# Masked attention weights in column blocks, a split copy of the first keys, and a new instruction list

## The chip, the cores and the metric

The kernel runs on one core of one Trainium2 chip. The metric is the device time of one execution in microseconds (us); lower is better. Five engines work side by side, each through its own instructions in program order: TensorE (PE in the profile; PEld are its weight loads), VectorE (DVE), ScalarE (ACT), GpSimd (POOL), and SyncE (SP), which issues most DMAs.

## The reference

A layer norm of x (2048 rows of 512) feeds two branches, whose outputs are added to x: an attention of 32 heads with a memory over four segments of 512 rows, and a dense layer with silu.

```python
xn = _layernorm(x, axis=-1)
return x + _A_ref(xn, A_wq, A_wk, A_wv, A_wo, A_beta) + _B_ref(xn, B_w1, B_w2)
# _A_ref, for each segment s of 4 (L = 512 rows, heads of 16 columns):
logits = jnp.einsum('bhqd,bhkd->bhqk', qs, ks) * scale + mask
p = _softmax(logits, axis=-1)
a_dot = jnp.einsum('bhqk,bhkd->bhqd', p, vs)
pq = phi(qs)
num = jnp.einsum('bhld,bhde->bhle', pq, M)
den = jnp.einsum('bhld,bhd->bhl', pq, z)[..., None] + 1e-06
o = g * (num / den) + (1.0 - g) * a_dot
pk = phi(ks)
M = M + jnp.einsum('bhld,bhle->bhde', pk, vs)
z = z + jnp.einsum('bhld->bhd', pk)
# _B_ref: silu(x @ w1) @ w2, with 1792 inner columns
```

The mask is `(row < column) * -1e9`: a query attends to keys up to its own row. phi(t) is t + 1 where t > 0, and exp(t) elsewhere.

## The kernel before

The whole program is one list of words, `ORDER`, written out by hand or by a search outside the kernel. Each word names a piece of work and is issued in that order; each engine then takes its own instructions in that order, held only by semaphores for data and buffers. `k0.1.2` is part 2 of the key product of segment 0, column tile 1; `q`, `v`, `h` and `o` (with the parts `oc`, `od`, `oh`) are the products of queries, values, the dense layer and the output. `S` is a batch of scores with its exponential and masks, `E` and `O` are the products of the weights with the values for the even and the odd half of each head pair. `ha` and `hv` are the tanh on ScalarE and the product on VectorE that make silu. In segments 0 and 1 a dense product of 512 columns has four parts of two matmuls of 256 columns, or of one of 512, about equal in length. These are the smallest pieces with which the list fills the time between two batches of scores.

Keys: `k_copy` (L370 on) copies the product of keys from PSUM to `kT` and then, on GpSimd, writes `k3`: the keys times a mask of the odd heads (512 columns) and, for half of the columns, of the even heads.

Scores: `scores` (L684 on) makes one of 72 batches. Nine batches serve each pair of column tiles in each segment. A batch holds one to two chunks, each a tile of 128 keys against all later queries, for four heads, and fills 512 columns of each of four PSUM banks (`psS`, of which there is one). One ScalarE operation (L707) writes the exponentials of all 2048 elements per partition as bf16 to a buffer `Pb`, of which six exist. GpSimd then sets to zero what the mask excludes (L718): for each chunk, the triangle of its first columns in place, and for the even half beforehand the lower rows of that triangle to a small buffer, `lows`.

```python
ONE = [[(0, 0, 0)], [(0, 0, 3), (0, 0, 1)], [(1, 0, 3), (1, 0, 0)], [(1, 0, 2), (1, 0, 1)]]
BATCHES = ONE + [[(0, 0, 2), (0, 1, 2)]] + [[(par, 1, kt) for par, _, kt in chunks] for chunks in ONE]
```

An entry is (half, tile of the pair, tile of keys). The lengths of the chunks are 512 - 128 kt columns in the even half and 64 less in the odd one. Batch 4 has two chunks of equal length, which one GpSimd operation masks; the two chunks of batches 1 to 3 and 6 to 8 differ in length and are masked one by one.

`weigh` (L746 on) multiplies the weights with the values (L763). As the next batch of scores writes the same four banks, its matmuls wait for the exponential of the batch before.

Prologue: four tiles of x are loaded, two on SyncE's and two on ScalarE's queue. Statistics on VectorE (L281, L284), a square root on ScalarE (L298) and a scaling (L310) give the normalized tile, which TensorE turns. 44 dummy matmuls (`busy44`, L836) and six more run meanwhile. `tb` (L304) loads ScalarE's table for the exponential ahead of its first use.

Of the kernel before, what the change touches and what calls it, by code (L numbers as in the profile page):

```python
# [8 lines left out]
AF = mybir.ActivationFunctionType  # L9
ALU = mybir.AluOpType  # L10
# [9 lines left out]
S1 Nv5 vv0.2 h0.5.0 h0.10.0 h0.10.1 h0.10.2 v0.3.3 vv0.3 xs8 Nv6 XD6 h0.5.1 h0.5.2 XD5 h0.5.3 ha0.5  # L20
S3 q0.3.0 q0.3.1 q0.3.2 q0.3.3 hv0.5 k0.2.0 qv0.3 Nv4 XD4 k0.2.1 k0.2.2 tanh h0.10.3 ha0.10
S4 fv0.0 k0.2.3 kv0.2 h0.11.0 h0.11.1 h0.11.2 h0.11.3 ha0.11 fv0.1 v1.3.0 v1.3.1 v1.3.2 v1.3.3
S7 vv1.3 hv0.10 h0.13.0 h0.13.1 fa0.3 h0.13.2 hv0.11 fp0.2 O0 E0 Ev0 Ov0
S5 v1.2.0 v1.2.1 v1.2.2 h0.13.3 ha0.13 v1.2.3 xs9 vv1.2 q1.1.0 q1.1.1 q1.1.2 q1.1.3 qv1.1 xs11
S11 Om0 v1.0.0 hv0.13 v1.1.0 v1.0.1 v1.0.2 v1.1.1 v1.0.3 h0.1.0 h0.1.1 h0.1.2 fp0.3 ga1.1
S6 vv1.0 v1.1.2 v1.1.3 xs10 lw0 xg8.4 h0.1.3 ha0.1 q1.2.0 t0.0 q1.2.1 q1.2.2 fv0.3 k1.2.0 vv1.1 k1.2.1 k1.2.2 k1.2.3 kv1.2
S8 q1.2.3 fa0.2 h0.2.0 h0.2.1 h0.2.2 h0.2.3 E1 qv1.2 gate hv0.1 h0.7.0
S9 q1.0.0 Ev1 fv0.2 t0.2 k1.1.0 k1.1.1 k1.1.2 Nv10 Nv11 h0.7.1 h0.7.2 h0.7.3 k1.1.3 kv1.1 ha0.7 hv0.7 q1.0.1 q1.0.2 Nv9 ha0.2 hv0.2
S10 h0.4.0 h0.4.1 XD10 t0.1 h0.4.2 h0.4.3 ha0.4 fp1.2 O1 Ov1 hv0.4 q1.0.3 h0.9.0 bmask qv1.0 gp1.0
S13 ga1.0 XD9 k1.3.0 h0.9.1 h0.9.2 k1.3.1 k1.3.2 xl0.2 h0.8.0 h0.8.1 xs13 h0.8.2 h0.8.3 k1.3.3 t0.3 kv1.3 ha0.8  # L30
S12 h0.12.0 h0.9.3 hv0.8 h0.12.1 h0.12.2 h0.12.3 ha0.12 k1.0.0 k1.0.1 XD11 k1.0.2 k1.0.3 Nv8 XD8 kv1.0 ha0.9 h1.11.0
S15 hv0.12 hv0.9 h1.11.1 h1.11.2 h1.11.3 ha1.11 E2 Ev2 O2 h1.9.0 h1.9.1
S17 Ov2 h1.9.2 h0.0.0 h0.0.1 hv1.11 o0.2.4 oc0.2.2.0 xs12 xs14 oc0.2.2.1 h1.9.3 ha1.9 hv1.9 o0.2.10 xs15 xg12.4 h0.0.2 oc0.2.9.1
S21 xl0.3 o0.2.1 q1.3.0 q1.3.1 o0.2.7 h0.0.3 q1.3.2 m0.2 ha0.0 o0.2.5 mv0.2 Om1 q1.3.3 qv1.3 hv0.0
S14 o0.2.11 h1.10.0 h1.10.1 gv1.0 Nv14 ga1.2 q2.1.0 o0.2.12 m0.0 mv0.0 q2.1.1
S16 qv2.1 h1.10.2 h1.10.3 gp1.2 h0.3.0 ha1.10 od0.2.0.2 h0.3.1 E3 h0.3.2 Ev3 h0.3.3 ha0.3 hv1.10
S19 hv0.3 h0.6.0 h0.6.1 h0.6.2 h0.6.3 ha0.6 O3 h1.0.0 Nv15 Ov3 h1.0.1 h1.0.2
S24 XD14 h1.0.3 k2.2.0 k2.2.1 Om2 hv0.6 v2.2.0 kv2.2 o0.2.3 gv1.2 oc0.2.9.0 sv0 ha1.0 hv1.0
S18 lw1 r0.1 v2.1.0 v2.1.1 r0.2 vv2.1 v2.2.1 vv2.2 o0.2.6 k2.1.0
S22 o0.2.13 k2.1.1 h1.8.0 kv2.1 h1.8.1 h1.5.0 h1.8.2 r0.0 h1.8.3 ha1.8 r0.3 XD15 w0 z0.0 h1.5.1  # L40
S20 z0.2 k2.0.0 hv1.8 z0.1 h1.5.2 h1.5.3 z0.3 gp1.1 k2.0.1 kv2.0 E4 Ev4 ha1.5 hv1.5 od0.2.0.3
S28 h1.4.0 h1.4.1 h1.4.2 q2.3.0 h1.4.3 ha1.4 q2.3.1 qv2.3 o0.0.9
S26 ga2.1 o0.0.1 oc0.0.13.0 od0.0.11.2 oc0.0.4.0 hv1.4 Nv12 O4 Ov4 q2.0.0 zv0.2 q2.0.1 qv2.0 zv0.0
S23 o0.0.2 XD12 h1.1.0 o0.0.16 h1.1.1 h1.1.2 od0.2.0.0 o0.2.16 h1.1.3 xl0.0 h1.12.0 ha1.1 od0.0.11.1 od0.0.11.0
S25 h1.12.1 h1.12.2 Om3 h1.12.3 od0.2.0.1 zv0.3 o0.0.14 oc0.0.4.1 hv1.1 gv1.1 o0.0.17 ha1.12 E5 Ev5 oc0.0.13.1
S29 o0.0.12 hv1.12 o0.0.8 od0.0.11.3 k2.3.0 zv0.1 k2.3.1 fa1.2 O5 kv2.3
S27 h1.6.0 mw0.0 fv1.2 o0.0.10 o0.0.6 t1.2 o0.0.5 gp2.1 h1.6.1 h1.6.2 o0.2.15 Ov5 h1.6.3 ha1.6 o0.0.0 hv1.6
S31 o0.0.7 o0.0.3 Nv13 XD13 o0.0.15 st0.0 o0.2.17 h1.13.0 h1.13.1 h1.13.2 h1.13.3 o0.2.8 ha1.13
S30 gv2.1 o0.1.17 od0.1.8.1 h1.3.0 h1.3.1 h1.3.2 h1.3.3 ha1.3 gp1.3 hv1.13 o0.1.6 od0.1.8.0 fp1.3 oc0.1.10.1 o0.1.3 hv1.3 o0.2.14 st0.2
S33 q2.2.0 oc0.1.10.0 o0.1.15 q2.2.1 qv2.2 o0.1.5 E6 fa1.3 fv1.3  # L50
S32 Ev6 o0.3.0 oc0.3.13.1 oc0.3.11.1 od0.3.10.3 oc0.3.11.0 o0.3.6 od0.1.8.2 o0.1.4 od0.3.10.2 mw0.2 Om5 od0.3.10.1 O6 t1.3 fa1.0 o0.3.15 Ov6
S35 od0.1.8.3 o0.1.13 oc0.3.13.0 o0.3.5 o0.3.12 o0.1.7 E7 Ev7 xl0.1 od0.3.10.0 ga1.3 oc0.1.12.0 o0.3.9 gv1.3 fp1.0 fv1.0 t1.0
S34 fp1.1 o0.1.0 v2.0.0 v2.0.1 vv2.0 h1.2.0 h1.2.1 fa2.3 o0.1.16 o0.3.17 Om6
S41 o0.3.8 o0.1.11 o0.1.1 O7 o0.1.14 oc0.1.12.1 fa1.1 o0.3.4 xl1.0 Ov7 o0.1.9
S37 o0.1.2 st0.1 h1.2.2 h1.2.3 o0.3.1 o0.3.3 o0.3.16 xl1.2 ha1.2 o1.2.4 od1.2.5.1 fv1.1 t1.1 m1.2 mv1.2 o1.2.1
S36 s1 hv1.2 o0.3.7 sv1 o0.3.2 fp2.0 r1.0 o0.3.14 st0.3 q3.1.0 q3.1.1 qv3.1 o1.2.12 fp2.3 fa2.0
S40 r1.1 v2.3.0 v2.3.1 vv2.3 h2.8.0 h2.8.1 r1.3 fv2.3 r1.2 ha2.8 hv2.8 q3.2.0
S43 q3.3.0 q3.3.1 qv3.3 w1 o1.2.8 q3.2.1 fa2.2 qv3.2 k3.1.0 d1.1 od1.2.5.2
S38 k3.1.1 kv3.1 z1.2 E8 Ev8 k3.0.0 k3.0.1 d1.2 m1.0 mv1.0
S42 h2.0.0 kv3.0 v3.3.0 xl1.1 od1.2.5.0 h2.0.1 ha2.0 v3.3.1 Om7 h1.7.0 fv2.0 vv3.3 d1.3  # L60
S39 fa2.1 hv2.0 h1.7.1 h1.7.2 h1.7.3 ha1.7 v3.0.0 v3.0.1 vv3.0 E9
# [32 lines left out]
def kernel(  # L94
# [820 lines left out]
```

## Time and profile before

| | |
|---|---|
| median of 3 runs | 222.32 us (222.01 to 222.53) |
| profiled execution | 222.15 us |
| its span | 220.4 us |
| granted TensorE clock, mean | 0.999 |
| exponentials (L707) | 72, 1878 ns each |
| masks on GpSimd (L718) | 120 in place, 56 to lows |

The span runs from the first to the last instruction; the profiled execution's own time is 1.75 us longer. A row of a timeline has the start, the length, the engine, the line, the operation and its operands (out<-in), how many instructions were merged (x), and in brackets how long the engine sat idle before it and what ended that. A row of the groups has the count, the busy time and the mean duration, and the idle time before. The lengths of matmuls overlap, since they are pipelined: their pace is read from start to start.

### The profile page before, as it was taken

What the parts mean: (1) busy time and instruction counts of PE and PEld (TensorE: products, weight loads), DVE (VectorE), ACT (ScalarE), POOL (GpSimd) and SP (SyncE); (2) the same over time, 40 slices, a digit from 0 to 9 for tenths busy, and PEclk for the clock granted to TensorE, in tenths of its full rate; (3) what the DMA queues carried; (4) which work ended last, traced back from release to release, by engine and by line L of the source; (5) the groups of instructions that cost most, each with busy time, mean ns of one, the idle gap of its engine ahead of it and who ended that gap; (6) DMA issues with size and microseconds to landing.
All of it is one profiled execution on the core that took longest, in us unless ns stands there. A gap on an engine that the chain in (4) does not pass through costs nothing.

```text
span 220.4 us, 9441 instructions
## 1 busy us (share of the span) xinstructions
PE 214.9 (97%) x4057; PEld 117.2 (53%) x4057; DVE 179.7 (82%) x368; ACT 184.0 (83%) x173; POOL 135.1 (61%) x253
## 2 busy tenths in 40 slices
PE   7999999999999999999999999999999999999994
PEld 7666645655553444454544444455454544455662
DVE  7789999988889788776897888969789887579554
ACT  3699999999999999999998999999989997971000
POOL 6089667997769976876669696693756364320000
PEclk9999999999999999999999999999999999999999
DMA  5993549552014221223303130142242020232313
GB/s 183 373 385 87 74 27 304 106 77 58 21 28 122 88 59 29 50 51 76 102 17 95 40 96 4 28 92 59 52 120 64 15 76 7 75 94 68 109 51 97
DMA packets 32746, 19.61 MB, mean 89 GB/s; under 512 B 14656, under 2 KB 32192, under 8 KB 32704
## 3 DMA queue, kind: packets, MB, share of 16 engines
q1 hardware_dynamic: 30080, 16.39, 28.6%
q10 hardware_dynamic: 2624, 2.62, 3.9%
q8 instruction: 31, 0.51, 1.0%
q14 instruction: 11, 0.09, 0.2%
HBM read 9.96 MB, written 2.10 MB: 55 GB/s over the span
## 4 chain that ended last, share of the span: by engine, by line
PE 79%; ACT 10%; DVE 4%; POOL 4%; issue 2%; POOLq 0%
PE ps L331 21%; PE psO L333 16%; PE ps L333 13%; PE psS L701 10%; PE psO L331 9%; ACT Pb L707 7%; PE psV L763 6%; PE psS L333 4%; POOL Pb L718 2%; DVE xn_t L310 1%; POOL lows L718 1%; ACT ex L408 1%; ACT th L477 1%; PE psM L437 1%; DVE stats L281 1%
## 5 line engine op out<-in xcount | busy, mean ns | idle before, releaser
L707 ACT ACTIVATE Pb<-psS 128x2048 bf16<-128x2048 f32 x72 | 135.2, 1878 | 7.5 <-PE psS L701 6.4
L718 POOL TENSOR_SCALAR_AFFINE_SELECT Pb<-Pb 128x256 bf16<-128x256 bf16 (+2 forms) x120 | 66.1, 571 | 22.3 <-ACT Pb L707 19.5
L482 DVE SCALAR_TENSOR_TENSOR hT<-th,ps 128x512 bf16<-128x512 bf16 x56 | 37.7, 679 | 9.1 <-ACT th L477 8.5
L718 POOL TENSOR_SCALAR_AFFINE_SELECT lows<-Pb 64x256 bf16<-64x256 bf16 (+1 forms) x56 | 26.7, 490 | 27.7 <-ACT Pb L707 25.3
L333 PE MATMUL psO<-w_sb,hT 128*32 128x512 bf16 (+2 forms) x716 | 42.5, 319 | 0.0
L331 PE MATMUL ps<-xnT,w_sb 128*128 128x512 bf16 (+1 forms) x160 | 35.2, 334 | 0.0
L477 ACT ACTIVATE th<-ps 128x512 bf16<-128x512 f32 x56 | 33.0, 598 | 2.2 <-PE ps L333 2.1
L333 PEld LDWEIGHTS <-hT 128*32 128x32 bf16 x884 | 21.8, 96 | 14.0 <-issue 3.3
L333 PE MATMUL ps<-xnT,w_sb 128*32 128x512 bf16 (+1 forms) x480 | 27.1, 341 | 0.1
L701 PE MATMUL psS<-qT,k 32*128 32x64 bf16 (+3 forms) x512 | 23.0, 233 | 0.8 <-ACT Pb L707 0.3
L331 PE MATMUL psO<-w_sb,hT 128*128 128x512 bf16 (+2 forms) x87 | 22.7, 334 | 0.0
L701 PEld LDWEIGHTS <-k 32*128 32x128 bf16 x512 | 9.8, 92 | 23.2 <-issue 21.7
L763 PE MATMUL psV<-Pb,Vz 128*32 128x448 bf16 (+7 forms) x512 | 21.6, 286 | 0.3 <-POOL Pb L718 0.3
L331 PEld LDWEIGHTS <-w_sb 128*128 128x128 bf16 x160 | 14.9, 98 | 12.1 <-issue 1.6
L763 PEld LDWEIGHTS <-Vz 128*32 128x32 bf16 x768 | 16.5, 97 | 9.1 <-issue 1.1
L376 POOL TENSOR_SCALAR k<-kT,pm_odd 128x512 bf16<-128x512 bf16 x16 | 12.0, 748 | 8.0 <-ACT kT L373 7.0
L333 PEld LDWEIGHTS <-w_sb 128*32 128x32 bf16 x480 | 11.9, 96 | 7.3 <-issue 1.9
L331 PE MATMUL ps<-wv_sb,xnT 128*128 128x512 bf16 x56 | 15.1, 381 | 0.2
L701 PE MATMUL psS<-qT,kT 16*128 16x448 bf16 (+3 forms) x256 | 14.7, 269 | 0.0
L333 PE MATMUL psO<-wo_sb,oT 128*32 128x512 bf16 x156 | 14.4, 380 | 0.0
L331 PE MATMUL ps<-xnT,wk_sb 128*128 128x256 bf16 (+1 forms) x64 | 13.6, 326 | 0.0
L793 DVE CAST oraw<-psV 128x512 bf16<-128x512 f32 x16 | 11.0, 689 | 3.0 <-PE psV L763 2.9
(110 smaller groups left out, 321.2 us busy)
## 6 DMA issues: line engine op xcount, KB each, us to landing
spr<-rz SPq DMA_DIRECT2D x56, 64.0 KB
x_res<-in_A_x_dram SPq DMA_DIRECT2D x16, 128.0 KB
out_dram<-o_out SPq DMA_DIRECT2D x15, 128.0 KB
w_sb<-in_B_w_dram SPq DMA_DIRECT2D x1, 1792.0 KB
w_sb<-in_B_w_dram ACTq DMA_DIRECT2D x1, 1792.0 KB
x_hi<-in_A_x_dram SPq DMA_DIRECT2D x2, 512.0 KB
wv_sb<-in_A_wv_dram SPq DMA_DIRECT2D x2, 256.0 KB
wk_sb<-in_A_wk_dram SPq DMA_DIRECT2D x1, 512.0 KB
```

What stands on the lines that cost most here:

```text
L281: nc.vector.bn_stats(out=stats[t][:], in_=xs(t, t + 1)[:, 0, :])
L310: eng.tensor_scalar(out=xn[t][:], in0=xs(t, t + 1)[:, 0, :], scalar1=mv_all[:, t, 0:1], scalar2=rstd_all[:, t, 0:1], op0=ALU.subtract, op1 ...
L331: return [nc.tensor.matmul(out, lhsT=lhsT, rhs=rhs, start=start, stop=stop, skip_group_check=True)]
L333: nc.tensor.matmul(out[c : c + 32], lhsT=lhsT[:, c : c + 32], rhs=rhs, start=start, stop=stop, tile_position=(0, c), skip_group_check=True,)
L376: nc.gpsimd.tensor_scalar(out=to, in0=frm, scalar1=keep[:, 0:1], scalar2=1.0, op0=ALU.mult, op1=ALU.mult)
L477: nc.scalar.activation(out=th[:], in_=sts[s]["h", ft][:, :], func=AF.Tanh, scale=0.5)
L482: nc.vector.scalar_tensor_tensor(out=st["hT"][:, ft, :], in0=st.pop(("th", ft))[:], scalar=1.0, in1=st.pop(("h", ft))[:, :], op0=ALU.add, ...
L701: nc.tensor.matmul(psS[:, g, c : c + q2 - q1], lhsT=keys[rows], rhs=st["qT"][rows, dt, q1:q2], start=True, stop=True, tile_position=(32 * ...
L707: exp = nc.scalar.activation(out=Pb[:, :, :], in_=psS[:, :, :], func=AF.Exp, scale=SCALE)
L718: over[id(Pb)].append(nc.gpsimd.affine_select(out=out, in_=in_, compare_op=ALU.is_ge, fill=0.0, base=base, pattern=[[0, out.shape[1]], [1, ...
L763: nc.tensor.matmul(psV[32 * g : 32 * g + 32, q0 : q0 + nq], lhsT=Vzs[s % 2][:, kt, 4 * dt + g, par : par + 2, :].rearrange("p a d -> p (a ...
L793: copy(out=oraw[:], in_=sts[s].pop(("psV", 0))[:, :])
```

## The change

1. Blocks. The weights of batches with two chunks of unlike length lie in `Pb` in blocks of columns, all four heads of a block together: 128 columns in batches 1 and 6, 64 in batches 2 and 7. The other batches stay as they are. The first blocks of the two chunks are then neighbours, and one GpSimd operation masks both (and one writes the lower parts of both). ScalarE writes the exponentials by blocks; the products with the values read them by blocks.
2. Prologue. Tile 0 of x is loaded in two halves on two queues. The small masks of odd and even heads are made later. The keys of tile 0 go through a new `k_fast`: ScalarE copies them, VectorE multiplies by the odd mask out of PSUM, and ScalarE multiplies half of them by the even mask out of PSUM. The table for the exponential is loaded earlier (`tb`), the first copy of queries moves to ScalarE, and 40 dummy matmuls replace 44.
3. The list `ORDER` is another one throughout.

```diff
-kind odd omask ones0 ones1 zeros xc0 xd0 xc1 xq0 xi0 Nv0 busy44 xd1 xq1 xc2 xi1 X0.1 Nv1 ... va0.0 va0.1 Nv3 Xv2.1 X3.1 Xv3.1 k0.0.0 k0.0.1 k0.1.0 k0.0.2 k0.0.3 k0.3.0 q0.0.0 q0.0.1 q0.0.2 q0.0.3 ka0.0 fp0.0 qv0.0 tb fa0.0 q0.2.0 k0.1.1 k0.1.2 k0.1.3 kv0.1 fp0.1
-S0 q0.1.0 q0.1.1 q0.1.2 q0.1.3 k0.3.1 xs4 xs6 xs7 xs5 xg4.4 q0.2.1 q0.2.2 qa0.1 q0.2.3 qv0.2
-S2 ...
+ones0 ones1 zeros xc0 xd0 xc1 xq0 xi0 Nv0 busy40 xd1 xq1 xc2 xi1 X0.1 Nv1 ... Nv2 X2.1 xi3 va0.0 Nv3 tb Xv2.1 X3.1 Xv3.1 k0.0.0 k0.0.1 odd kind va0.1 k0.3.0 k0.0.2 k0.0.3 kf0.0 q0.0.0 q0.0.1 q0.0.2 q0.0.3 qa0.0 k0.3.1 fa0.0 k0.3.2 k0.3.3
+S0 v0.3.0 q0.3.0 q0.3.1 q0.3.2 xs5 xs6 xs7 xs4 xg4.4 k0.1.0 k0.1.1 k0.1.2 k0.1.3 ka0.1 q0.3.3 qv0.3
+S2 ...
...
-    load_x(nc.sync, 0, 1)
+    load_x(nc.sync, 0, 1, slice(0, P // 2))
+    load_x(nc.scalar, 0, 1, slice(P // 2, P))
     load_x(nc.scalar, 1, 1)
     load_x(nc.sync, 2, 1)
     load_x(nc.scalar, 3, 1)
...
+    def k_fast(s, dt):
+        kT, (odd, even) = k_tiles(s, dt)
+        ps = sts[s].pop(("k", dt))
+        k_in = ps[:, :].rearrange("p (t c) -> p t c", c=P)
+        nc.scalar.copy(out=kT, in_=ps[:, :])
+        nc.vector.tensor_scalar(out=odd, in0=k_in, scalar1=pm_odd[:, 0:1], scalar2=None, op0=ALU.mult)
+        nc.scalar.activation(out=even, in_=k_in[:, :, 0:HP], func=AF.Copy, scale=pm_even[:, 0:1])
...
+    BLOCK = [L, 2 * HP, HP, L]
+    BLOCK = BLOCK + [L] + BLOCK
+
+    def blocks(Pb, b):
+        return Pb[:, :, :].rearrange("p g l -> p (g l)").rearrange("p (y g c) -> p y g c", g=4, c=BLOCK[b])
...
-        exp = nc.scalar.activation(out=Pb[:, :, :], in_=psS[:, :, :], func=AF.Exp, scale=SCALE)
+        exp = nc.scalar.activation(
+            out=blocks(Pb, b).rearrange("p y g c -> p g y c"),
+            in_=psS[:, :, :].rearrange("p g (y c) -> p g y c", c=BLOCK[b]), func=AF.Exp, scale=SCALE,
+        )
...
-        for first, out in zip(firsts, to):
-            select(out[0:HP], first[HP:P, :, 0:HP], 0)
-        for first in reversed(firsts):
-            select(first[:, :, 0:P], first[:, :, 0:P], 0)
+        select(low[0:HP, :].rearrange("p (n c) -> p n c", c=HP), firsts[HP:P, :, 0:HP], 0)
+        select(firsts[:, :, 0:P], firsts[:, :, 0:P], 0)
...
+            w = BLOCK[b]
+            ys, cs = (slice(c0 // w, (c0 + nq) // w), slice(0, w)) if w < L else (slice(0, 1), slice(c0, c0 + nq))
+            weights = blocks(st["Pb", pair, b], b)[:, ys, :, cs].rearrange("p y g c -> p g y c")
...
-                    rhs=weights[:, g, :],
+                    rhs=weights[:, g, :, :],
```

More of the change, by code (lines that the diff above doesn't have):

```diff
@@ L20 @@
[L20 to L25, printed above, removed]
@@ L366, in k_mm, with k_tiles, k_copy @@
         dense(s, "k", wk_sb, dt, part)
-    def k_copy(s, dt, copy=nc.vector.tensor_copy):
+    def k_tiles(s, dt):
         kT = seg_tile(s, "kT")
         k3 = sts[s]["k3", dt] = segp.tile([P, TPS, 3 * HP], BF16, name="k3", bufs=6)
-        copy(out=kT[:, dt, :], in_=sts[s].pop(("k", dt))[:, :])
-        k_in = kT[:, dt, :].rearrange("p (t c) -> p t c", c=P)
-        for to, frm, keep in ((k3[:, :, HP : 3 * HP], k_in, pm_odd), (k3[:, :, 0:HP], k_in[:, :, 0:HP], pm_even)):
+        return kT[:, dt, :], (k3[:, :, HP : 3 * HP], k3[:, :, 0:HP])
+    def k_copy(s, dt, copy=nc.vector.tensor_copy):
+        kT, (odd, even) = k_tiles(s, dt)
+        copy(out=kT, in_=sts[s].pop(("k", dt))[:, :])
+        k_in = kT.rearrange("p (t c) -> p t c", c=P)
+        for to, frm, keep in ((odd, k_in, pm_odd), (even, k_in[:, :, 0:HP], pm_even)):
             nc.gpsimd.tensor_scalar(
@@ L724, in scores @@
         if even:
-            firsts = [Pb[:, :, :].rearrange("p g (x c) -> p (g x) c", c=2 * P)]
-            to = [low[:, :].rearrange("p (n c) -> p n c", c=HP)]
-            read = low[:, :].rearrange("p (g x c) -> p x g c", x=2, c=HP)
-        else:
-            firsts = [Pb[:, :, PLACE[chunk][1] :] for chunk in BATCHES[b]]
-            if low is not None:
-                read = low[:, :].rearrange("p (x g c) -> p x g c", g=4, c=HP)
-                to = [read[:, x, :, :] for x in range(len(firsts))]
+            firsts = Pb[:, :, :].rearrange("p g (x c) -> p (g x) c", c=2 * P)
+            read = low[:, :].rearrange("p (g x c) -> p x g c", x=2, c=HP) if low is not None else None
+        elif BLOCK[b] < L:
+            firsts = blocks(Pb, b)[:, 0:2, :, :].rearrange("p y g c -> p (y g) c")
+            read = low[:, :].rearrange("p (x g c) -> p x g c", g=4, c=HP) if low is not None else None
+        elif low is not None:
+            firsts = Pb[:, :, :]
+            read = low[:, :].rearrange("p (x g c) -> p x g c", g=4, c=HP)
         if low is None:
-            for first in firsts:
+            chunks = [firsts] if BLOCK[b] < L else [Pb[:, :, PLACE[chunk][1] :] for chunk in BATCHES[b]]
+            for first in chunks:
                 select(first[:, :, 0:HP], first[:, :, 0:HP], HP)
@@ L759, in weigh @@
                 x = BATCHES[b].index((0, d, kt))
[L760 removed]
+                parts.append((kt, st["low", pair, b][1][:, x, :, :].unsqueeze(2), kt * P, HP))
         for i, (kt, weights, q0, nq) in enumerate(parts):
```

152 lines of the change are left out of this document (79 added, 73 removed).

## The prediction, made before the changed kernel ran

> **What bounds the kernel now.** I read the page first (busy time by engine, the chain that ended last), then the timelines of ScalarE (ACT), GpSimd (POOL) and TensorE (PE) in the first 25 us, then the groups of instructions by shape.
>
> ```profile
> PE 214.9 (97%) x4057; PEld 117.2 (53%) x4057; DVE 179.7 (82%) x368; ACT 184.0 (83%) x173; POOL 135.1 (61%) x253
> ...
> PE 79%; ACT 10%; DVE 4%; POOL 4%; issue 2%; POOLq 0%
> ```
>
> TensorE is busy for 97% of the span and carries 79% of the chain. GpSimd, which the change relieves most, carries 4%. The instruction order of the two programs shows that TensorE has the same columns to stream in both, apart from four of the 44 first dummy matmuls, which fill a wait for the first normalized tile: the same score, value, dense and output products, with the same 72 turns into the scores' row tiling and back. So the end moves only with what TensorE loses: how late its real work starts, and how long it waits. The 10% of ACT in the chain are mostly at the head; here is why:
>
> ```profile
> 8.16 0.58 ACT L391 CAST Vz<-ps 128x512 bf16<-128x512 f32 x1
> 8.93 0.59 ACT L391 CAST Vz<-ps 128x512 bf16<-128x512 f32 x1 [0.19 <-PE ps L331]
> 10.60 0.59 ACT L373 CAST kT<-ps 128x512 bf16<-128x512 f32 x1 [1.08 <-PE ps L331]
> 11.20 1.28 ACT L304 ACT_TABLE_LOAD   x1
> 12.50 0.20 ACT L304 ACTIVATE spare<-eps 128x1 f32<-128x1 f32 x1
> 12.61 0.61 ACT L408 ACTIVATE ex<-kT 128x512 bf16<-128x512 bf16 x1
> 13.13 1.86 ACT L707 ACTIVATE Pb<-psS 128x2048 bf16<-128x2048 f32 x1
> ```
>
> ```profile
> 11.29 0.70 POOL L376 TENSOR_SCALAR k<-kT,pm_odd 128x512 bf16<-128x512 bf16 x1 [7.01 <-ACT kT L373]
> 11.97 0.48 POOL L376 TENSOR_SCALAR k<-kT,pm_even 128x256 bf16<-128x256 bf16 x1
> ```
>
> The first exponential (ACT L707) waits for the first scores, and these for the masked keys: a copy on ACT, then two multiplies on POOL. From there on scores and exponentials alternate, because the four banks of scores exist once. The first scores and those of two later batches on TensorE:
>
> ```profile
> 12.51 0.21 PE L701 MATMUL psS<-qT,k 32*128 32x64 bf16 x4
> ...
> 15.04 0.40 PE L701 MATMUL psS<-qT,k 32*128 32x64 bf16 x8 [0.28 <-ACT Pb L707]
> ...
> 19.81 0.40 PE L701 MATMUL psS<-qT,k 32*128 32x192 bf16 x8
> 20.14 1.05 PE L331 MATMUL ps<-xnT,wq_sb 128*128 128x256 bf16 x8
> 21.03 0.82 PE L331 MATMUL ps<-xnT,wk_sb 128*128 128x256 bf16 x6
> 21.68 0.38 PE L331 MATMUL ps<-xnT,w_sb 128*128 128x256 bf16 x2
> 22.19 0.21 PE L701 MATMUL psS<-qT,k 32*128 32x64 bf16 x4
> ```
>
> From one batch of scores to the next it is 2.38 us (19.81 to 22.19). Eight matmuls of 256 columns take 0.89 us (20.14 to 21.03), so 0.11 each, and one "piece" of the list, two of them, 0.22. Between these scores stand 16, which start at 20.14 and are through by 21.92; about 0.2 us is lost to the exponential. A gap needs nine pieces to cover it; the old list has eight in three of the first five gaps.
>
> **The change part by part.** Durations are those of the profiled execution: it took 222.15 us, 1.75 more than its span of 220.4; the median of the runs is 222.32, 0.17 above it.
>
> *The head.* Two rows bear on it:
>
> ```profile
> 3.65 0.70 DVE L281 BATCH_NORM_STATS2 stats<-x_lo 128x6 f32<-128x512 bf16 x1
> ...
> 12.57 0.69 DVE L373 CAST kT<-ps 128x512 bf16<-128x512 f32 x1 [0.18 <-PE ps L331]
> ```
>
> Tile 0 of x now comes in halves on two queues, and the small masks leave VectorE's (DVE's) queue ahead of the first statistics at 3.65. I take 0.2 us for it. No row prices a half load; it cannot make things later than one queue alone would by more than a little, and the bounds are 0 and 0.5. The ACT table load goes between the two copies of Vz: from 11.20 to 12.61 it and its dummy cost 1.41, so the second copy ends near 8.74 - 0.2 + 1.41 + 0.59 = 10.54, about when the key products are done (10.60 - 0.2). The table load thus leaves the path. But the new fast copy of keys has three readers of one PSUM tile: ACT copies it, DVE multiplies by the odd mask, ACT multiplies half of it by the even mask. In the changed program DVE's multiply waits for ACT's copy and ACT's second operation for DVE's, so they run in turn, and the copy of the queries, now on ACT, stands behind them. From 10.55: 0.59 for the copy, 0.1 handover (11.19 to 11.29 in POOL's row), 0.69 on DVE (its cast of the same shape out of PSUM), 0.1 handover, about 0.38 on ACT for half the columns (between a third and all of 0.59: 0.2 to 0.59), 0.59 for the queries, 0.05: first scores at 13.05 instead of 12.51. That is 0.55 later; with the bounds from 0.2 to 0.9 later. DVE has nothing queued that runs into this; on ACT the exponential of the keys (0.61) follows and is as near to the first Pb as before.
>
> The Trainium skill, "PSUM — Partial Sum Buffer", section "PSUM bank collisions raise a hardware error", says that two engines may not access one bank's quadrant at once, reads against reads included. It speaks against the split: by it nothing is won by sharing the copy between engines, and the sum is the serial one above; no run here shows a collision. Had the three run together, the first scores would stand at 10.55 + 0.59 + 0.38 + 0.59 + 0.05 = 12.16, and the sum below would be 0.9 lower.
>
> Before the first scores the new list places 20 pieces of dense work where the old one places 22. Two pieces, 0.44 us, are then still to be done: together the head costs +0.99. In the new list seven pieces, 1.54 us, follow the last key product, against a chain of 2.5: TensorE idles about 1 us ahead of the first scores.
>
> *The list after the head.* Nine pieces stand in each of the next gaps where the old one has eight, so waits of 0.2 for exponentials (the row of 15.04 has 0.28) go in three gaps, and the first shrinks to about 0.1. Another kind of wait:
>
> ```profile
> 39.06 1.08 ACT L477 ACTIVATE th<-ps 128x512 bf16<-128x512 f32 x2
> 40.02 1.90 ACT L707 ACTIVATE Pb<-psS 128x2048 bf16<-128x2048 f32 x1
> ```
>
> Where two tanh stand in one gap, the next exponential comes about 0.4 us later after its scores (1.08 against the 0.5 that fit), and the gap after it needs eleven pieces. I laid both lists out gap by gap: TensorE's columns between scores, and ACT's operations, against the pitch of 2.38. Old: 0.9 us of such waits in the first six gaps, 0.85 in the others. New: 0.35 and 0.35, since gaps with two tanh are followed by longer ones. That is -1.05; it can't be better than -1.75, and if the new list's gaps are broken by waits that I don't see, it is 0.
>
> *Fewer, larger masks.* By shape:
>
> ```profile
> L718 POOL TENSOR_SCALAR_AFFINE_SELECT Pb<-Pb 128x512 bf16<-128x512 bf16 x48 | 30.9, 661 | 2.2
> L718 POOL TENSOR_SCALAR_AFFINE_SELECT Pb<-Pb 128x256 bf16<-128x256 bf16 x64 | 26.5, 438 | 19.5 <-ACT Pb L707 19.5
> L718 POOL TENSOR_SCALAR_AFFINE_SELECT lows<-Pb 64x256 bf16<-64x256 bf16 x48 | 20.5, 442 | 22.8 <-ACT Pb L707 20.6 <-PE ps L331 1.3
> ...
> L718 POOL TENSOR_SCALAR_AFFINE_SELECT Pb<-Pb 128x1024 bf16<-128x1024 bf16 x8 | 8.7, 1093 | 0.5
> ```
>
> In 16 batches two operations of 661 ns become one of 1093: 16 x 0.23 = 3.7 us. In 16 others two of 438 become one of 661: 16 x 0.215 = 3.4 us. The lower parts (442 ns each) merge likewise, for a little more. POOL loses over 7 of 135 us, all of it beside TensorE's work except where the value products wait for a mask:
>
> ```profile
> 48.74 0.79 POOL L718 TENSOR_SCALAR_AFFINE_SELECT Pb<-Pb 128x256 bf16<-128x256 bf16 x2
> ...
> 49.58 0.40 PE L763 MATMUL psV<-Pb,Vz 128*32 128x320 bf16 x8 [0.26 <-POOL Pb L718]
> ```
>
> Here TensorE idled 0.26; by the gap table some 0.3 more goes in this way elsewhere. Chains from exponential to products get 0.2 to 0.35 shorter, and the new list leaves about as much TensorE work as the old between scores and the products that read them. I take -0.5, with bounds of 0 and -0.7.
>
> *The blocks.* ACT now writes 32 of the 72 weights in runs of 64 or 128 columns, and the products read them so.
>
> ```profile
> L384 ACT CAST qT<-ps 128x512 bf16<-128x512 f32 x2 | 1.2, 586 | 0.0
> L391 ACT CAST Vz<-ps 128x512 bf16<-128x512 f32 x2 | 1.2, 586 | 0.2 <-PE ps L331 0.2
> ```
>
> ```profile
> L763 PE MATMUL psV<-lows,Vz 128*32 128x64 bf16 x256 | 4.7, 193 | 0.0
> ...
> L437 PE MATMUL psM<-Vz,phiK 128*32 128x32 bf16 x192 | 2.4, 177 | 0.0
> ```
>
> The copy into Vz writes runs of 16 and costs the same 586 ns as the plain one. A product that reads two runs of 16 (psM) is 16 ns shorter than one of 64 columns in one run. Both say nothing is added: 0. No row has eight runs of 64, so the other end stays open (a rival below).
>
> Sum: 0.55 + 0.44 - 1.05 - 0.5 = -0.56 us: 221.6 for a profiled execution, and from the median of 222.32 about **221.8 us**.
>
> **The rivals.** *The list also takes waits that I left in.* TensorE's waits in the old list add to about 3 us by the gap table; I take away 1.05 + 0.5. If the new one is near free of them, another 0.9 goes: 220.9. For: POOL and DVE have more room. Against: a list is made before it runs, and the late first scores show one place where it doesn't fit.
>
> *The late head is not made up* (slower). The three readers hand over more slowly than POOL's 0.1, at 0.2 to 0.3 each, and the first scores come at 13.5: +1.0 and +0.44. Everything behind them was placed for scores that come earlier: ACT takes the second key copy and tanh late, the gaps stretch over 2.38, and of the 1.05 some 0.3 is won, of the 0.5 some 0.2. Sum +0.95: 223.3. It decides from the point where scores later than 13.4 meet savings below 0.9 in the gaps. For: about 1 us of idle TensorE that the list didn't fill with ready products. Against: the pitch of 2.38 was held in the old one over many batches.
>
> *The blocks cost.* If the 32 exponentials were 0.1 longer each, most of 3.2 us would show in the exponential-paced stages: about 224.5. The two ACT rows speak against it.
>
> That the masks are merged without any use to the end is within the forecast: then POOL's 0.5 is missing and it is 222.3.
>
> **How the numbers follow.** Forecast 0.50, range of its own 221.2 to 222.5; waits taken too 0.20; late head 0.24; blocks 0.06. A measurement of this kernel tells 0.2% (0.44 us) from no change: below 221.88 is faster, above 222.76 slower. The forecast lies close to the first edge: of its 0.50 I give 0.27 to faster, 0.16 to same, 0.07 to slower. So faster 0.47, same 0.16, slower 0.37. The range from 220.6 to 223.4 leaves out the blocks' case and the ends of the first and third.
>
> **What would show it.** In the changed profile: first scores at 13.0 +- 0.2, TensorE idle for about 1 us before them, DVE's k between two ACT operations; scores 2.38 apart in the next gaps without a wait for Pb; masks of 128x1024 near 1093 ns, POOL near 127 us; exponentials still 1878 ns for all shapes; the end of TensorE near 216.7. I am wrong if the first scores come before 12.3 or after 13.5, if the exponentials of blocked batches differ, or if value products wait for masks, queries or sums for over 1 us in all.

## The result and the profile after

| | before | after |
|---|---|---|
| median of 6 runs (us) | 222.16 (221.99 to 222.53) | 225.35 (224.53 to 226.07) |
| profiled execution, its span (us) | 222.15, 220.4 | 225.07, 223.3 |
| first scores, start of the last four matmuls (us) | 12.51, 217.27 | 13.50, 219.57 |

The changed kernel is slower: the ratio is 1.0141, with a 95% interval of 1.0112 to 1.017. The forecast was 221.8 us, with a range from 220.6 to 223.4. The runs after also lie further apart, 1.5 us against 0.5. From the page of the kernel after, the busy time and the chain that ended last:

```profile
PE 215.3 (96%) x3990; PEld 117.2 (52%) x3990; DVE 180.8 (81%) x368; ACT 185.4 (83%) x175; POOL 125.9 (56%) x203
...
PE 76%; POOL 8%; DMA 6%; ACT 3%; issue 2%; DVE 2%; SPq 1%; DVEq 0%; POOLq 0%; ACTq 0%
```

GpSimd has lost 9.2 us of work, and yet its share of the chain has doubled, from 4% to 8%; DMA, which was not named before, carries 6%. ScalarE, which carried 10%, carries 3%. So what releases TensorE has changed. The groups by shape say that the pieces themselves cost about what was expected:

```profile
L744 POOL TENSOR_SCALAR_AFFINE_SELECT Pb<-Pb 128x1024 bf16<-128x1024 bf16 x24 | 26.7, 1110 | 1.6
...
L730 ACT ACTIVATE Pb<-psS 128x2048 bf16<-128x2048 f32 x72 | 135.2, 1878 | 9.4 <-PE psS L724 7.8
```

Who waited for whom on TensorE (in all, times, longest), before the change:

```profile
PE psS L836 <- DVE zraw L183: 1.1, 1, 1.1
PE psS L701 <- ACT Pb L707: 0.3, 1, 0.3
PE psV L763 <- POOL Pb L718: 0.3, 1, 0.3
PE ptr L817 <- DVE xn_t L310: 0.2, 1, 0.2
```

and after it:

```profile
PE ps L333 <- DVE hT L497: 1.2, 1, 1.2
PE psS L864 <- DVE zraw L185: 1.1, 1, 1.1
PE psV L791 <- POOL Pb L744: 1.0, 2, 0.7
PE psS L724 <- ACT qT L399: 0.5, 1, 0.5
PE ps L333 <- DMA wk_sb<-in_A_wk_dram: 0.3, 1, 0.3
PE ps L333 <- DMA wq_sb<-in_A_wq_dram: 0.2, 1, 0.2
```

Apart from the first 1.1 us, which both kernels have ahead of the dummy matmuls, four waits are new, and the one for GpSimd's masks has grown from 0.3 to 1.0. The one for an exponential is gone, as forecast. Three places hold the new waits; a fourth loss lies behind TensorE's last matmul.

**The head.** TensorE, ScalarE and VectorE in the timeline after:

```profile
9.80 1.26 PE L333 MATMUL ps<-xnT,wk_sb 128*128 128x256 bf16 x10 [0.26 <-DMA wk_sb<-in_A_wk_dram]
11.10 0.58 ACT L391 CAST kT<-ps 128x512 bf16<-128x512 f32 x1 [0.20 <-PE ps L333]
11.26 0.61 PE L333 MATMUL ps<-xnT,wq_sb 128*128 128x256 bf16 x4 [0.20 <-DMA wq_sb<-in_A_wq_dram]
11.72 0.75 DVE L392 TENSOR_SCALAR k<-ps,pm_odd 128x512 bf16<-128x512 f32 x1 [0.88 <-ACT kT L391]
12.50 0.47 ACT L393 ACTIVATE k<-ps,pm_even 128x256 bf16<-128x256 f32 x1 [0.82 <-DVE k L392]
12.88 0.58 ACT L399 CAST qT<-ps 128x512 bf16<-128x512 f32 x1
13.50 0.21 PE L724 MATMUL psS<-qT,k 32*128 32x64 bf16 x4 [0.54 <-ACT qT L399]
```

The three readers of the keys run in turn, and from the first copy to the first scores it is 2.40 us (11.10 to 13.50); the forecast had 2.5. What was wrong is where this chain starts: at 11.10, not at 10.55. The key product waited for the weights wk, and the query product for wq. SyncE's first loads of x now take 1.46 us to issue instead of 0.86 to 0.87, so those of wk and wq are issued 0.6 later:

```profile
0.79 1.46 SPq L158 DMA_DIRECT2D x_lo<-in_A_x_dram  x2
```

**Masks near 29 us.** GpSimd, and the product that waits for it:

```profile
24.86 1.01 POOL L382 TENSOR_SCALAR k<-kT,pm_odd 128x512 bf16<-128x512 bf16 x1
25.85 0.50 POOL L382 TENSOR_SCALAR k<-kT,pm_even 128x256 bf16<-128x256 bf16 x1
26.31 0.78 POOL L744 TENSOR_SCALAR_AFFINE_SELECT Pb<-Pb 128x256 bf16<-128x256 bf16 x2
27.88 2.15 POOL L744 TENSOR_SCALAR_AFFINE_SELECT Pb<-Pb 128x1024 bf16<-128x1024 bf16 x2
29.02 0.29 PE L791 MATMUL psV<-Pb,Vz 128*32 128x256 bf16 x4 [0.66 <-POOL Pb L744]
```

The products of `E0` read batch 4, whose mask is the first of the two at 27.88. Its exponential had ended at 25.8. But GpSimd was still busy with the keys of tile 2 (`kv0.2`, 1.5 us from 24.86), which no scores need before segment 0's second pair. The same happens once more at 49.13, with 0.33.

**The sums near 70 us.** VectorE, the DMA issues (SPq, ACTq) and TensorE after:

```profile
63.86 1.04 SPq L813 DMA_DIRECT2D zraw<-odd  x2
64.34 0.38 ACTq L170 DMA_DIRECT2D wo_sb<-in_A_wo_dram  x1
68.52 0.66 DVE L521 TENSOR_SCALAR zsum<-zraw,evec 128x256 f32<-128x256 bf16 x1 [1.46 <-DMA wo_sb<-in_A_wo_dram]
69.21 1.38 DVE L545 RECIPROCAL ri<-zsum 128x64 f32<-128x64 f32 x3
70.73 0.68 DVE L497 SCALAR_TENSOR_TENSOR hT<-th,ps 128x512 bf16<-128x512 bf16 x1
71.47 1.02 PE L333 MATMUL ps<-xnT,wq_sb 128*128 128x512 bf16 x4 [1.23 <-DVE hT L497]
```

and the same three steps before:

```profile
62.88 1.04 SPq L785 DMA_DIRECT2D zraw<-odd  x2
65.68 0.51 DVE L506 TENSOR_SCALAR zsum<-zraw,evec 128x256 f32<-128x256 bf16 x1
65.68 0.41 ACTq L168 DMA_DIRECT2D wo_sb<-in_A_wo_dram  x1
```

The word `sv0` reads the softmax sums, which two small copies of 2 KB bring to `zraw`. Before, it could read them 1.76 us after their issue had ended (63.92 to 65.68), with no wait shown. In the new list the load of wo (`lw1`, 512 KB) stands one gap ahead of `sv0` instead of just behind it, at the head of the next gap; its issue falls beside those of the small copies, and the sums are there only 3.6 us after theirs (64.90 to 68.52). VectorE's queue stands: three reciprocals and the silu product `hT` are behind it, and the query product needs the bank that `hT` frees. The Trainium skill, "DMA: Bandwidth & Descriptors", section "Issuing engines are not separate DMA queues", says that transfers issued by different engines run on the same 16 DMA engines and interleave. The rows above fit it: the copies from SyncE's queue were readable only 3.6 us after their issue, with a load from ScalarE's queue issued beside them. Experiments 3 and 12 test whether the load is the reason.

**The end.** The prediction let the end move only with TensorE. But the last four matmuls start 2.30 us later than before, and the span is 2.9 longer. Before, VectorE's last addition waits for its product; after, the last two wait for stores:

```profile
217.61 0.42 DVE L653 SCALAR_TENSOR_TENSOR o_half<-psS,x_res 128x256 bf16<-128x256 f32 x1 [0.17 <-PE psS L333]
```

```profile
219.46 0.69 DVE L621 SCALAR_TENSOR_TENSOR o_out<-psO,x_res 128x512 bf16<-128x512 f32 x1 [0.55 <-DMA out_dram<-o_half]
220.33 0.42 DVE L668 SCALAR_TENSOR_TENSOR o_half<-psS,x_res 128x256 bf16<-128x256 f32 x1 [0.17 <-DMA out_dram<-o_out]
```

In the kernel `o_out` and `o_half` share three buffers, so an addition can write only when the store of the third addition before it has landed. From the start of the last four matmuls to the end of the span it is 3.2 us in all three profiles with the old list, and 3.7 to 4.1 in all eleven with the new one.

### The profile page after: what moved, and what is told of

Same layout as the page of the kernel before. It is cut to its first block, busy times and chain, and to the rows that moved or that the text cites. A ratio compares the mean times of both kernels' runs of the same rounds, so it can differ in the third digit from the quotient of the medians.

```text
span 223.3 us, 9263 instructions
## 1 busy us (share of the span) xinstructions
PE 215.3 (96%) x3990; PEld 117.2 (52%) x3990; DVE 180.8 (81%) x368; ACT 185.4 (83%) x175; POOL 125.9 (56%) x203
## 4 chain that ended last, share of the span: by engine, by line
PE 76%; POOL 8%; DMA 6%; ACT 3%; issue 2%; DVE 2%; SPq 1%; DVEq 0%; POOLq 0%; ACTq 0%
PE ps L333 18%; PE psO L335 14%; PE ps L335 13%; PE psO L333 10%; PE psS L724 9%; PE psV L791 7%; PE psS L335 3%; DMA wk_sb<-in_A_wk_dram 3%; POOL Pb L744 3%; POOL k L382 2%; ACT Pb L730 2%; DMA wo_sb<-in_A_wo_dram 2%; POOL lows L744 2%; DMA out_dram<-o_out 1%; POOL pos L417 1%
## 5 line engine op out<-in xcount | busy, mean ns | idle before, releaser
L744 POOL TENSOR_SCALAR_AFFINE_SELECT Pb<-Pb 128x512 bf16<-128x512 bf16 (+2 forms) x88 | 62.6, 721 | 22.8 <-ACT Pb L730 20.1
L744 POOL TENSOR_SCALAR_AFFINE_SELECT lows<-Pb 64x512 bf16<-64x512 bf16 (+1 forms) x40 | 22.8, 569 | 47.1 <-ACT Pb L730 40.1
L335 PE MATMUL psO<-w_sb,hT 128*32 128x512 bf16 (+2 forms) x628 | 39.5, 321 | 0.0
L333 PE MATMUL ps<-xnT,w_sb 128*128 128x512 bf16 (+1 forms) x163 | 33.5, 334 | 0.0
L333 PE MATMUL psO<-w_sb,hT 128*128 128x512 bf16 (+2 forms) x109 | 27.2, 329 | 0.0
L335 PEld LDWEIGHTS <-hT 128*32 128x32 bf16 x796 | 20.1, 97 | 12.9 <-issue 2.6
L335 PE MATMUL ps<-xnT,w_sb 128*32 128x512 bf16 (+1 forms) x468 | 26.0, 341 | 0.1
L333 PEld LDWEIGHTS <-hT 128*128 128x128 bf16 x109 | 9.9, 98 | 10.3 <-issue 1.7
L333 PE MATMUL ps<-wv_sb,xnT 128*128 128x512 bf16 x50 | 14.0, 386 | 0.0
L333 PE MATMUL ps<-xnT,wq_sb 128*128 128x256 bf16 (+1 forms) x58 | 11.8, 321 | 1.4 <-DVE hT L497 1.2
```

The costliest lines, as they stand in the source:

```text
L333: return [nc.tensor.matmul(out, lhsT=lhsT, rhs=rhs, start=start, stop=stop, skip_group_check=True)]
L335: nc.tensor.matmul(out[c : c + 32], lhsT=lhsT[:, c : c + 32], rhs=rhs, start=start, stop=stop, tile_position=(0, c), skip_group_check=True,)
L744: over[id(Pb)].append(nc.gpsimd.affine_select(out=out, in_=in_, compare_op=ALU.is_ge, fill=0.0, base=base, pattern=[[0, out.shape[1]], [1, ...
```

## The experiments

All times are medians; ratios are to the kernel before, run on the same chip beside them, with 95% intervals. The kernel before itself ran at 222.16, 222.4, 222.49 and 222.15 in the four rounds (the result; experiments 1 to 4; 5 to 8; 9 to 12). So where a run is compared with the changed kernel, which was measured in the first round alone, the ratios are the better guide.

**1. Blocks alone.** The changed code with the old list and the old prologue.

```diff
-ORDER (new), x tile 0 in two halves
+ORDER (old), x tile 0 in one load
```

> The old list and the old prologue, word for word, with the blocks and the merged masks. Theory: the 3.2 us by which the changed kernel is slower come from the new list alone (late head, a wait for masks near 29 us, a wait for the sums' transfer near 70 us), and blocks cost nothing: 221.9 us (221.6 to 222.3), exponentials 1878 ns, GpSimd near 127 us. Rival: writing or reading the weights in blocks costs TensorE or ScalarE something that the groups don't show: 223.5 or more.

222.08 us; 0.9991 (0.9975 to 1.0008). From its groups by shape:

```profile
L729 ACT ACTIVATE Pb<-psS 128x2048 bf16<-128x2048 f32 x72 | 135.2, 1878 | 6.9 <-PE psS L723 5.7
```

Blocks cost nothing, and under the old list merged masks bring little or nothing. The loss is in the list and the prologue.

**2. The list and the prologue alone**, with the old layout and each chunk masked by itself.

```diff
-blocks(Pb, b), merged selects
+Pb[:, :, :], one select for each chunk
```

> The new list and the new prologue with the weights in one run of 512 columns and each chunk masked alone, as before the change. Theory: the new list needs the merged masks; without them GpSimd's queue ahead of the first value products grows by about 0.6 us and other waits for masks appear: 226.3 us (225.8 to 227.5). Rival (blocks cost): faster than the changed kernel, 224 or less.

228.08 us; 1.0259 (1.0221 to 1.0296). The theory holds, and by more than it said: the new list needs the merged masks. Without them it is some 2.6 us slower still, by the two ratios.

**3. The load of wo behind the sums.**

```diff
-S24 lw1 v2.2.0 v2.2.1 ...
-S18 sv0 r0.0 r0.3 ...
+S24 v2.2.0 v2.2.1 ...
+S18 sv0 lw1 r0.0 r0.3 ...
```

> The changed kernel with the load of wo issued behind the reading of the sums (one gap later) instead of one gap ahead of it. Theory: the small copies to zraw, issued at 63.9 to 64.9 us, land late only because 512 KB of wo are under way; zsum then starts by 67.2 instead of 68.5, the 1.2 us wait of the query products at 71.5 is gone, and the time falls from 225.35 to 224.1 (223.8 to 224.5). Rival: the sums land at 68.3 whatever else is loaded, since they were issued late: 225.3, and zsum at 68.5.

224.69 us; 1.0101 (1.007 to 1.0132). Its timeline:

```profile
57.85 1.02 PE L333 MATMUL ps<-xnT,wk_sb 128*128 128x512 bf16 x4 [0.71 <-DMA x_res<-in_A_x_dram]
...
64.63 1.04 SPq L813 DMA_DIRECT2D zraw<-odd  x2
67.51 0.38 ACTq L170 DMA_DIRECT2D wo_sb<-in_A_wo_dram  x1
67.76 0.34 DVE L521 TENSOR_SCALAR zsum<-zraw,evec 128x256 f32<-128x256 bf16 x1
```

`zsum` starts without a wait, and the 1.23 us of the query product are gone. The time fell by 0.7 only (0.9 by the ratios), where 1.25 was expected. In this execution another wait stands ahead: the first key product of segment 2, at 57.85, waits for its turned tiles (`XD8`, `XD10`; the row names the transfer issued last). The changed kernel's profile doesn't have it. The new list reads those tiles 3 us after their issue, and how late they land differs from run to run.

**4. Key masks later.** GpSimd's multiplies of two key tiles moved behind the masks that the value products wait for.

```diff
-S1 ... k0.2.3 kv0.2 ...          -S12 kv1.3 ...
+S1 ... k0.2.3 kc0.2 ...          +S12 kc1.3 ...      # kc: the copy alone
-S7 ... E0 Ev0                    -S17 q1.3.0 ...
+S7 ... E0 Ev0 km0.2              +S17 km1.3 q1.3.0 ... # km: GpSimd's multiplies
```

> The changed kernel with GpSimd's two key multiplies of segment 0, tile 2 (1.5 us at 24.9) put behind the masks of the batch that the first value products read, and those of segment 1, tile 3 likewise behind the masks near 48 us. Theory: the waits of the value products at 29.0 and 49.1 us (0.85 and 0.5 us of idle TensorE) go: 224.2 us (223.8 to 224.7). Rival: GpSimd is behind by more than these multiplies, the wait moves to the odd half's products or to later scores: 225.0 or more.

224.85 us; 1.0109 (1.0077 to 1.0141): 0.5 less than the changed kernel, 0.7 by the ratios, about half of the 1.15 that was expected. Batch 4's mask and the scores behind `E0` in its timeline:

```profile
26.22 1.09 POOL L750 TENSOR_SCALAR_AFFINE_SELECT Pb<-Pb 128x1024 bf16<-128x1024 bf16 x1
27.65 0.21 PE L730 MATMUL psS<-qT,k 32*128 32x64 bf16 x4
```

The mask comes 1.66 us earlier, of which the head of this execution gives 0.56, and the wait for it is gone. At 49 us I had moved the wrong keys: tile 3 of segment 1 lies behind the mask in question, tile 0 ahead of it, and the wait stayed.

**5. Keys of tile 0 by GpSimd**, as before the change (`kf0.0` becomes `ka0.0`).

> The changed kernel, with only the keys of tile 0 masked as before the change: ScalarE's copy, then two GpSimd multiplies, instead of the three readers in turn. Theory: the three readers cost the chain from the key product to the first scores; with GpSimd (0.70 and 0.48 us) beside ScalarE's copy of the queries the first scores come 0.3 to 0.5 earlier than in the changed kernel, and the time falls from 225.35 to about 225.0. Rival: the late weights (wk, wq) set the first scores and the way the keys take is hidden: same first scores, 225.3.

225.39 us; 1.013 (1.0104 to 1.0157): little or no gain, though the first scores come at 12.61, 0.9 earlier. Most of these 0.9 aren't the keys': in this execution the key product starts at 9.03 instead of 9.80, and from there to the first scores it is 3.58, against 3.70. Its timeline shows where the rest of the gain went:

```profile
18.43 0.61 PE L333 MATMUL ps<-xnT,w_sb 128*128 128x256 bf16 x4 [1.40 <-DMA w_sb<-in_B_w_dram]
```

The new list starts the dense layer one gap earlier than the old one, and the load of its weights (1792 KB, issued at 4.89) lands at 18.38 here. What came earlier waited there. In the changed kernel's profile this wait is absent, in that of experiment 2 it is 0.44.

**6. Tile 0 of x in one load**, the rest of the prologue as changed.

> The changed kernel, with only tile 0 of x loaded as before the change, in one transfer on SyncE's queue. Theory: the halves gain 0.3 us for the statistics but put a transfer ahead of the others on both queues; with one transfer the weights wk and wq land earlier, the waits of the key and query products for them (0.26 and 0.20 us in the changed kernel) go, and the first scores come at about the same time or 0.2 earlier: 225.2. Rival: the halves gain what they were made for, and without them all comes 0.3 later: 225.7.

225.14 us; 1.0115 (1.009 to 1.0139): 0.2 less than the changed kernel, 0.6 by the ratios. The first scores come at 12.92, more than expected, and one part of the theory is wrong:

```profile
3.31 0.69 DVE L282 BATCH_NORM_STATS2 stats<-x_lo 128x6 f32<-128x512 bf16 x1 [0.68 <-DMA x_lo<-in_A_x_dram]
```

The statistics start at 3.31; with the halves it was 3.37. So the halves gained nothing; what the statistics gained over 3.65 came from the small masks that left VectorE's queue. The halves only put the weights' issue back: here wk is issued at 2.68, and the key product starts at 9.14 without a wait. Whether a late issue leads to a wait differs between executions: in experiment 4 wk is issued at 3.27, and the key product starts at 9.11 without a wait too.

**7. The old prologue** with the new list from the first scores on.

> The changed kernel with the whole prologue as before the change (one load of tile 0, 44 dummy matmuls, small masks first, GpSimd's key masks, the table load after the copies), the rest of the new list as it is. Theory: the head is 0.8 to 1.0 us of the 3.2: first scores near 12.5 instead of 13.5, 224.5 us (224.2 to 224.8). Rival: earlier scores only move the time into the later waits, for masks at 29 us and for the sums at 70 us, which go by GpSimd's and the transfers' pace: 225.2, with a longer wait at 28 us.

224.81 us; 1.0102 (1.0079 to 1.0124): first scores at 12.81, and 0.5 won, 0.9 by the ratios, so that the two cases can't be told apart by the time; the waits of 1.0 for masks and 1.2 behind the sums are still there.

**8. All of these together, first try**: the old prologue, the load of wo behind the sums, key masks behind the masks (in segment 1 those of tile 0), and the first key product of segment 2 moved to the end of its gap.

> The changed kernel with the old prologue, the load of wo behind the reading of the sums, the key masks of segment 0, tile 2 and of segment 1, tile 0 put behind the masks that the products at 29 and 49 us wait for, and the first key product of segment 2 moved to the end of its gap, behind the landing of its transposes. Theory: these four places hold the whole loss (0.9 + 1.2 + 0.85 + 0.5, and what varies from run to run at 57 us), and the paced waits stay away: 221.6 us (221.0 to 222.2), with a spread of the runs like the old kernel's 0.5. Rival: the new list is slower in many small places besides: 222.8 or more.

224.92 us; 1.0114 (1.0078 to 1.015). A miss, and of my own making:

```profile
54.02 0.40 PE L729 MATMUL psS<-qT,k 32*128 32x192 bf16 x8 [2.00 <-POOL k L387]
```

The keys of segment 1, tile 0, whose masks I had put into the gap of `S17`, are read by the very next scores, `S21`. If nothing else had taken up this wait, the profiled execution of 223.92 us would have been near 221.9.

**9. Together, mended.** Lines of experiment 8 (-) and of this one (+):

```diff
-S17 km1.0 q1.3.0 ...      -S14 h0.6.1 h0.6.2 h0.6.3 ... k2.2.0 k2.2.1 kv2.2
+S13 km1.0 h0.12.3 ...     +S14 h0.6.1 h0.6.2 k2.2.0 k2.2.1 h0.6.3 ... kv2.2
-S2 ... Nv5 h0.5.0 Nv7 XD7 h0.10.0
+S2 ... Nv5 k0.2.0 Nv7 XD7 k0.2.1
-S1 h0.10.1 ... h0.11.0 ... ha0.5 hv0.5 k0.2.0 k0.2.1 k0.2.2 k0.2.3 kc0.2
+S1 k0.2.2 k0.2.3 kc0.2 h0.5.0 ... ha0.5 hv0.5 h0.10.0 h0.10.1 h0.11.0
```

> The earlier mended version with two of its own mistakes taken back: the key masks of segment 1, tile 0 now come behind the masks of the batch that the products at 49 us read, but ahead of the first scores of segment 1 (which waited 2.0 us for them); the first key product of segment 2 moves back by two pieces of its gap only. And two pieces of the keys of tile 2 change places with the first two pieces of the dense layer, which in one run waited 1.4 us for the load of w1. Theory: the loss sits in these few waits; without them 221.6 us (221.0 to 222.2). Rival: the list loses in many small places: 222.8 or more.

221.97 us (221.63 to 222.35); 0.9991 (0.9981 to 1.0). TensorE's waits, as the profile lists them:

```profile
PE psS L869 <- DVE zraw L184: 1.1, 1, 1.1
PE psS L729 <- POOL k L387: 0.4, 1, 0.4
PE psV L796 <- POOL Pb L749: 0.2, 1, 0.2
```

3.4 us are back (3.3 by the ratios), by moving a dozen words of the list and undoing the prologue. Almost all that TensorE lost sat in these places; the end, which no experiment changes, still costs 0.5 in this profile (217.62, with 0.52 of waiting for a store). The runs lie 0.7 us apart, not 1.5. Against the kernel before it is at best 0.2% faster.

**10. The same with the changed prologue.**

> As mended2, but with the changed prologue (halves of tile 0, three readers of the first keys) instead of the old one. Theory: first scores near 13.3 instead of 12.4, and since nothing behind absorbs it, 0.8 us more than mended2: 222.4. Rival (the prologue only shifts waits): the same as mended2.

222.59 us; 1.0013 (1.0001 to 1.0024): 0.6 more than experiment 9, with first scores at 13.35 against 12.81. By this, nothing behind absorbs the later head. Its profile has 0.4 for the turned tiles of segment 2 besides, so not all of the 0.6 need be the prologue's.

**11. The same without blocks.**

> As mended2, with the weights in one run of 512 columns and each chunk masked alone. Theory: the merged masks matter under this list, which leaves less time between the exponentials and the products that read them, 1 to 2 us more than mended2: 223.1. Rival: once GpSimd's key masks are out of the way, merged masks are worth no more than in the old list: 221.9, 0.3 more than mended2.

223.01 us; 1.0037 (1.0023 to 1.005), 1.0 more than experiment 9. Its waits for masks:

```profile
PE psV L782 <- POOL Pb L737: 0.7, 3, 0.3
```

Merged masks are worth 1 us under this list, at most 0.6 under the old one (by the interval of experiment 1).

**12. The old kernel with the load of wo one gap earlier.**

```diff
-S24 XD14 ...      -S18 lw1 r0.1 ...
+S24 lw1 XD14 ...  +S18 r0.1 ...
```

> The kernel before the change, with only the load of wo moved one gap forward, ahead of the reading of the sums. Theory: the copies to zraw issued at 62.9 to 63.9 us then land behind the load; zsum starts at about 67.3 instead of 65.7, VectorE's next operations stand behind it, and part of this reaches TensorE: 222.9 us (222.5 to 223.4). Rival: the wait needs the new list's place for the sums too: 222.3, zsum at 65.7.

224.0 us; 1.0102 (1.0062 to 1.0142). One word moved costs the old kernel 1.85 us by the medians, more than expected; the ratio takes in one run of 227.01. The copies' issue ended at 63.80 here, so the sums were read 3.8 us after it:

```profile
67.63 0.35 DVE L506 TENSOR_SCALAR zsum<-zraw,evec 128x256 f32<-128x256 bf16 x1 [1.99 <-DMA zraw<-odd]
68.64 0.59 PE L331 MATMUL ps<-xnT,wk_sb 128*128 128x512 bf16 x2 [1.51 <-DVE hT L482]
```

## Why the prediction was wrong

**The head: the step from the copy of Vz to the first keys failed.** The chain of three readers was right (2.40 against 2.5), and so was that they run in turn: VectorE starts 0.04 after ScalarE's copy ends, ScalarE 0.03 after VectorE. The term took the key product as done at 10.60, less 0.2 because x came earlier. But the halves, priced as a gain of 0.2 that could hardly turn into a loss, gained nothing and put the weights' issue back by 0.6, and in this execution the product waited for them. The head is 0.99 later in the profile, not 0.55. In experiment 4, with the same late issue, the weights came in time, and its chain starts and ends about as forecast (10.55 and 13.05), with the first scores at 12.94:

```profile
10.53 0.59 ACT L397 CAST kT<-ps 128x512 bf16<-128x512 f32 x1
```

Between that product and the one of the changed kernel lie 0.69 us (9.11 and 9.80). The wait for wk is the larger part, some 0.42; the other, 0.27, was there before it, since the last turned tiles came at 8.90 instead of 8.63. There TensorE itself was slow. The six dummy matmuls ahead of the first real products (`busy6`) took 0.50 us before the change and in experiment 4, and 0.85 here (first the row of before, then that of after):

```profile
5.94 0.50 PE L836 MATMUL psS<-zraw 128*128 128x128 bf16 x6
```

```profile
5.83 0.85 PE L864 MATMUL psS<-zraw 128*128 128x128 bf16 x6
```

This differs between executions, with 44 dummies ahead as with 40, and the profile's granted clock reads 1.00 in all these slices, so it doesn't show why. The spread with the old prologue goes with it: of seven profiles, five have these six in 0.50 and first scores between 12.28 and 12.51, two (experiments 7 and 9) in 0.66 and 0.82 and first scores at 12.81. The five profiles with the changed prologue stand between 12.94 and 13.50. In the time the prologue costs up to 0.6 (experiments 9 and 10). The two pieces of 0.44 were not measured alone.

**The waits for exponentials: the sign was right, the size was not measured alone.** The scores after the head stand exactly 2.40 apart (13.50, 15.90, 18.30), and no wait for `Pb` on ScalarE is left in the list of waits. But experiment 9, which has the old prologue and none of the large new waits, should by the remaining terms stand 0.44 - 1.05 - 0.5 = -1.1 from the kernel before. It stands at -0.2. Most of the missing 0.9 lies elsewhere. From the first scores to the last four matmuls it is 204.76 us before, and 203.97 in experiment 9 (12.81 to 216.78), 203.80 in experiment 10: the gains of the list and the masks are there, at 0.8 to 1.0 of the 1.1. In the profile of experiment 9, 0.3 is lost ahead of this stretch, where its first scores came at 12.81, and 0.5 behind it.

**The end: the step "the end moves only with what TensorE loses" failed.** From the start of the last four matmuls to the end of the span it is 3.16 before and 3.70 after, 0.54 more, where the sum had nothing. That the reuse of three buffers sets it stands on the kernel and on the rows, which name a store in eight of the eleven profiles with the new list; no run changes the end alone.

**The masks: the term had the wrong sign.** GpSimd's busy time was forecast at 127 and is 125.9, and a mask of 1024 columns takes 1110 ns, as forecast. The failing step was "the new list leaves about as much TensorE work as the old between scores and the products that read them". I compared TensorE's side only, and did not lay out GpSimd's queue: what stands in it ahead of each mask that a product reads. There the key multiplies of tile 2 had moved ahead of batch 4's mask, and the wait went from 0.3 to 1.0. Experiments 2 and 11 show that the merged masks by themselves are a gain: 2.6 us under the new list, 1.0 under its mended form.

**Transfers: there was no term at all.** I laid out two engines' queues and took each transfer as landed. `lw1` and `sv0` had changed places, which can be seen in the list. It cost TensorE 1.23 in the profile; made alone in the old kernel (experiment 12), it cost TensorE 1.51 in the profile and the kernel 1.85 by the medians. The other two landings, that of w1 at 18.4 (none to 1.40) and that of turned tiles at 57.9 (none to 0.97), differ between executions; that they make the larger spread is suggested by experiment 9, where both have more room, and not shown by itself.

**The blocks were free**, as forecast; the rival that they cost is refuted by experiment 1. Of the rivals, the late head had the right sign, and its first scores at 13.5 came true to the digit, but by luck: it made them late by handovers of 0.2 to 0.3 us between the three readers, which took 0.03 to 0.04. Its time, 223.3, is 2 us short. The condition "value products wait for masks, queries or sums for over 1 us in all" is the one that came true: 1.0 and 1.2.

The single repairs of experiments 3, 4 and 7 brought 0.5 to 0.7 each by the medians, 0.7 to 0.9 by the ratios, and their intervals overlap that of the changed kernel; that each wait was real stands on the rows, and on experiment 9. They don't add up singly, since a wait that is taken out uncovers the next landing (experiments 3 and 5).

## What to carry to other kernels

When a list of work is reordered, lay out every queue, those of DMAs too, and for each reader the distance from the issue of what it reads; the engine that is busiest shows only which waits matter, not who causes them. Keep a large load from being issued between a small transfer and its reader: here one word's place was worth 1.85 us. Look behind the last matmul too: what is stored there may have to wait for a buffer. And when a change that relieves an engine makes the kernel slower, run the parts crossed (old list with new code, new list with old code) before looking for a cost in the code.

## What was not expected of the hardware

Copies of 2 KB, readable within 1.8 us of their issue, took 3.6 and 3.8 us (the changed kernel and experiment 12) when 512 KB issued from another engine were under way, though they were issued beside it and not behind it.

A GpSimd multiply of the same shape took 0.69 to 1.01 us (at 20.43 and 24.86 in the kernel after), and at 24.86 an operation of VectorE beside it was long too:

```profile
25.24 0.77 DVE L312 TENSOR_SCALAR xn_t<-x_hi,mv_all,rstd_all 128x512 bf16<-128x512 bf16 x1
```

An operation of this kind and shape takes 0.41 at 8.68, where GpSimd is idle. The Trainium skill, "SBUF — State Buffer", section "SBUF: two separate sides", says that VectorE, in some modes or with two inputs from SBUF, and GpSimd lock a pair of ports against each other. These rows fit that, but no run here tested it, and at 20.43, where GpSimd took 0.69, VectorE was at work too. Either way, the mean of GpSimd's multiplies of this shape is 0.78, so a queue laid out from it was 0.23 too short at 24.86.
